# A planner that counts a longer landing time for the loads and stores of weights that are made early

## The chip, the core and the metric

The kernel runs on one core of a Trainium2 chip. The metric is the device time of one execution in microseconds; less is better. In the profile PE is TensorE (matmul), DVE is VectorE, ACT is ScalarE, POOL is GpSimd and SP is SyncE, whose queue issues every DMA of this kernel.

## What is computed

A banded attention with block summaries, a gated feed-forward network and a second network with a tanh residual, one after the other, in fp32 (cut to what matters):

```python
# attention: batch 2, 8 heads, 768 positions, head size 64; blocks of 32, window 16
k_sum = k.reshape(B, H, nb, block, D).max(axis=3)
v_sum = v.reshape(B, H, nb, block, D).mean(axis=3)
scores_l = np.where(abs(i - j) < window, scale * q @ k.T, -1e9)
scores_s = scale * q @ k_sum.T + log(block)
attn = softmax(concat(scores_l, scores_s)) @ concat(v, v_sum)
# feed-forward 1: 1536 tokens, 512 -> 1536 -> 512
xn = x / rms(x) * rms_g
x = (silu(xn @ w_gate) * (xn @ w_val)) @ w_out
# feed-forward 2: 512 -> 2048 -> 512
h = x @ w_in
out = (h - tanh(h)) @ w_out2
```

The weights of both networks come as 8-byte floats and are turned to fp32 on the chip.

## The kernel before

**Work.** The 1536 tokens are twelve tiles of 128, in three groups of four. Attention is done in 24 units (a tile and half of the heads). The first network (kind "a") goes over the three groups, each with twelve steps, one for each 128 columns of the hidden layer; a step is 4 + 4 first products (gate and value, into the PSUM tiles `mid`) and 4 second products (into the accumulators `bank`). Every fp32 product is three matmuls (L778 to L780) of rounded parts, high and low: `ih`, `il` for gate and value weights, `oh`, `ol` for the out weights, `hh`, `hl` for the hidden values. The units of the next group run between the steps of the one before. The second network (kind "b") takes the hidden columns in eight pairs for each group: seven products with added and subtracted blocks in place of eight, then the second products.

**Weights.** `widen` (L720) loads 8-byte weights into one of two `raw` buffers (L734) and turns them into fp32 with ACT (L736) and DVE (L737, L738). `split` makes the rounded parts, high by ACT (L753) and low by DVE or POOL (L755). For the second network's out weights `make_out` (L994) does both early, during the first network's second group: load into `raw` (L1002), ACT L1004, DVE L1005 and L1006, then the high part by ACT (L1007) and the low part by DVE or POOL (L1011) into the one buffer `op` (printed as `hi`), and two stores of 256 KB to device memory (L1015, tensors `ko`). There are sixteen such weights, so 16 loads and 32 stores; the next L1007 can't write `op` before both stores have landed. The second network later fetches the parts again (`fetch_outs`, L1020) into `oh` and `ol`, of which there are three each, shared with the first network's splits. `make` does the like for the second network's first weights (tensors `ki`, L1060 to L1082).

**What sets the order.** Nothing is written in the order in which it runs. Every instruction is an `Op` with an engine, an estimated time, the operations that it comes after, the buffers (`Slot`) that it takes, and a due time. `Plan.order` runs a clock over them: on each engine the ready operation with the smallest latest start is taken next, if its buffers are free. The order that comes out is written into the engines' instruction streams, and each engine then works strictly in that order on the chip, waiting by semaphores. A wrong estimate therefore breaks nothing, but lets an engine stand before an instruction whose input is not there while later ones could run. A DMA of `mb` MB is estimated at `mb * 2.78` us (L371); `lag` (L98) adds 1.0 us until its reader may start, and 1.3 us between an engine's end and a DMA. A buffer counts as free for an engine 0.2 us (`LAT`) after its last user's end, for a DMA 1.3 us after.

Of the kernel before, what the change touches and what calls it, by code (L numbers as in the profile page):

```python
# [16 lines left out]
NT, DM = B * S, H * D  # L17
# [3 lines left out]
P = 128  # L21
# [29 lines left out]

OPS = 7
AHEAD = 20.0
GROWS = (slice(32, 64), slice(64, GROW + 2 * NB))


def r32(ap):
    return ap.bitcast(F32)
# [11 lines left out]
class Op:  # L70
    def __init__(self, eng, us, fn, after, slots, due, rank, port):
# [5 lines left out]
        self.after = [o for o in after if o is not None]  # L77
        self.start = self.late = None


class Plan:

# [14 lines left out]

    def lag(self, a, b):  # L98
        if a.eng == "dma":
            return 0.0 if b.eng == "dma" else 1.0  # L100
        if b.eng == "dma":
            return 1.3
        if a.eng == b.eng:
            return {"pe": 0.0, "dve": 0.13}.get(a.eng, 0.05)
        return self.LAT

    def order(self, filler=None, gap=0.0):
# [58 lines left out]
        while events:  # L166
# [3 lines left out]
            for eng, queue in list(ready.items()):  # L170
# [28 lines left out]
                for s in o.slots:  # L199
                    if s.pool and s.index is None:  # L200
                        t, s.index = s.pool.idle.pop(0)
                        if s.most:
                            s.pool.held += 1
                    s.left -= 1
                    if s.pool and not s.left:
                        insort(s.pool.idle, (end, s.index))
                        insort(events, end + self.LAT)
                        insort(events, end + 1.3)
                        if s.most:
                            s.pool.held -= 1  # L210
                for q in o.then:
# [45 lines left out]
def kernel(  # L257
# [109 lines left out]
        o.alts = dict(rest)  # L367
        return o

    def dma(mb, fn, *after, **kw):  # L370
        return plan.op("dma", mb * 2.78, fn, after, **kw)  # L371

    def cols(tl, t):
        for i, (t0, n) in enumerate(GROUPS):
# [42 lines left out]
    def summary(b, hb, *after):  # L417
# [3 lines left out]
        def load(dst, src, rank):  # L421
            parts = 2 if b else 1
            n = NP * S // parts
            return [
                dma(
                    n * P * 4e-6,
                    lambda c=slice(j * S + i * n, j * S + i * n + n): nc.sync.dma_start(dst[:, c], src[:, c]),
                    *after,
                    rank=None if b else rank + 3 * hb,
                )  # L430
                for i in range(parts)
            ]
# [62 lines left out]
    def one_unit(t, hb, due, tag="att"):  # L495
# [7 lines left out]


        def load_part(c, rank=None):
            return dma((c.stop - c.start) * P * 4e-6, lambda: nc.sync.dma_start(u[:, c], units[i, :, c]), slots=[u], rank=rank)

        if i < 2:
            load = load_part(slice(0, VO), (-99, -96.65)[i])
# [467 lines left out]
    def dma_both(n, pick, slots, kept, *after):  # L977

        ops = []
        for s, k in zip(slots, kept):  # L980
            def go(s=s, k=k):
                here, there = r32(s[:, :n]), r32(k)
                nc.sync.dma_start(*((here, there) if pick else (there, here)))

            o = dma(n * P * 4e-6, go, *after, chain.get(("ld", n == DM)) if pick else None, slots=[s])
            if pick:
                chain["ld", n == DM] = o
            ops.append(o)
        return ops
# [4 lines left out]
    def make_out(f, due):  # L994
# [4 lines left out]
        du = lambda: d[:].bitcast(U32)  # L999
        src = w2[f].bitcast(U32)  # L1000
        gate = first_ops["a", 0]
        ld = dma(0.524, lambda: nc.sync.dma_start(raw[:], src[:, 1024:2048]), chain.get("raw"), slots=[raw])  # L1002
        chain["raw"] = ld
        a = act(0.58, lambda: nc.scalar.activation(d[:], w(1).bitcast(F32), AF.Prelu, scale=2.0 ** -112, alpha=-(2.0 ** 32)), ld, *gate, slots=[raw, d])  # L1004
        a = dve(0.34, lambda: nc.vector.tensor_scalar(du(), du(), 3, None, ALU.logical_shift_left), a, slots=[d], port=True)  # L1005
# [4 lines left out]
        def rest(on):  # L1010
# [1 line left out]

        z = flex({"pool": (1.32, lambda: rest(nc.gpsimd), True), "dve": (0.61, lambda: rest(nc.vector), True)}, a, slots=[d, o])
        stored_o[f] = [
            dma(DM * P * 4e-6, lambda i=i: nc.sync.dma_start(r32(keep_o[n][j][i]), o[:, i * 512:(i + 1) * 512]), x, slots=[o], due=due)  # L1015
            for i, x in enumerate((a, z))
        ]
        made_o.extend(stored_o[f])
# [1 line left out]
    def fetch_outs(n):  # L1020
        outs = []
        for j in (1, 0):
            w = [slot("oh"), slot("ol")]
            o = dma_both(DM, True, w, keep_o[n][j], *stored_o[2 * n + j])
            outs.insert(0, (*w, [o]))
        return outs

# [328 lines left out]
```

## Time and profile before

| | |
|---|---|
| median of 3 runs | 673.54 us (670.91, 673.54, 906.21) |
| the profiled execution | 674.08 us, its span 672.4 us |
| PE busy | 656.7 us (98%), 3714 matmuls |
| DVE busy | 451.4 us (67%) |
| ACT busy | 333.1 us (50%) |
| POOL busy | 48.9 us (7%) |
| DMA | 136.51 MB, mean 203 GB/s |

The span is the time from the first to the last instruction of the profiled execution. Busy time is the union of an engine's instructions; the ends of matmuls are modelled, so what a matmul costs is better read from the distance of starts. A wait is an engine's idle time together with the instruction, or the DMA, that ended it.

### The profile page before, as it was taken

Reading aid. Unit: us, or ns where it says so; the run is one execution under the profiler, and the core shown is the slowest. Engines: PE = TensorE matmul, PEld = TensorE weight load, DVE = VectorE, ACT = ScalarE, POOL = GpSimd, SP = SyncE. Lnnn points to the kernel's source line nnn. Section 1 sums busy time; section 2 is a strip of 40 time slices with the busy share of each in tenths; the row PEclk is TensorE's granted clock in tenths of the full one; section 3 lists DMA queues with packets and bytes.
Section 4 is the critical chain, followed back from the end, with each engine's and each line's share of the span. In section 5 each row is a group of like instructions: output and inputs, shape, how many; then the busy total and the mean of one; then the engine's idle time right before and its main releaser. Section 6 shows DMA issues by size and latency. Waiting matters only on the chain.

```text
span 672.4 us, 10478 instructions
## 1 busy us (share of the span) xinstructions
PE 656.7 (98%) x3714; PEld 552.6 (82%) x3714; DVE 451.4 (67%) x1011; ACT 333.1 (50%) x688; POOL 48.9 (7%) x114
## 2 busy tenths in 40 slices
PE   8999999999999999999999999999999999999996
PEld 7997777888876778888878888888888888888885
DVE  5798987885876875549978547987583444445343
ACT  3995566774764755447645436444362222323222
POOL 2221222110112120000000000000000000000000
PEclk9999999999999999999999999999999999999999
DMA  9886564662477665000645017687768787888842
GB/s 342 325 298 238 177 203 145 194 197 84 129 236 245 204 200 202 0 1 1 234 157 157 0 68 294 235 304 272 253 230 288 267 282 267 282 305 276 268 167 94
DMA packets 52251, 136.51 MB, mean 203 GB/s; under 512 B 6200, under 2 KB 8680, under 8 KB 52200
## 3 DMA queue, kind: packets, MB, share of 16 engines
q1 hardware_dynamic: 52200, 135.86, 60.2%
q8 instruction: 29, 0.48, 0.3%
q14 instruction: 22, 0.18, 0.1%
HBM read 109.62 MB, written 26.21 MB: 202 GB/s over the span
## 4 chain that ended last, share of the span: by engine, by line
PE 58%; DMA 4%; DVE 4%; ACT 2%; issue 1%; SPq 0%; DVEq 0%; ACTq 0%
PE bank L778 12%; PE bank L780 12%; PE bank L779 12%; PE mid L778 7%; PE mid L779 6%; PE mid L780 6%; DMA raw<-in_w_dram 3%; DMA out_dram<-th 1%; PE bank L641 1%; DMA ko<-hi 1%; PE bank L547 1%; PE bank L598 1%; DVE wd L738 1%; PE bank L652 0%; ACT wd L736 0%
## 5 line engine op out<-in xcount | busy, mean ns | idle before, releaser
L778 PE MATMUL mid<-hi,ih 128*128 128x512 f32 (+1 forms) x304 | 121.7, 400 | 0.1
L779 PE MATMUL mid<-lo,ih 128*128 128x512 f32 (+1 forms) x304 | 116.7, 384 | 0.0
L780 PE MATMUL mid<-hi,il 128*128 128x512 f32 (+1 forms) x304 | 116.5, 383 | 0.0
L780 PE MATMUL bank<-oh,hl 128*128 128x512 f32 x192 | 75.7, 394 | 0.5 <-DVE hl L1164 0.5
L778 PE MATMUL bank<-oh,hh 128*128 128x512 f32 x192 | 75.9, 395 | 0.1
L779 PE MATMUL bank<-ol,hh 128*128 128x512 f32 x192 | 75.4, 392 | 0.0
L778 PEld LDWEIGHTS mid<-hi,ih 128*128 128x128 f32 x304 | 57.4, 189 | 12.8 <-issue 2.4
L780 PEld LDWEIGHTS mid<-hi,il 128*128 128x128 f32 x304 | 57.2, 188 | 12.1
L779 PEld LDWEIGHTS mid<-lo,ih 128*128 128x128 f32 x304 | 57.4, 189 | 9.8
L778 PE MATMUL bank<-hh,oh 128*128 128x512 f32 (+1 forms) x152 | 60.3, 397 | 0.0
L779 PE MATMUL bank<-hl,oh 128*128 128x512 f32 (+1 forms) x152 | 58.2, 383 | 0.9 <-DVE hl L839 0.9
L780 PE MATMUL bank<-hh,ol 128*128 128x512 f32 (+1 forms) x152 | 58.1, 382 | 0.0
L753 ACT CAST ih<-wd 128x512 fp32r<-128x512 f32 x76 | 46.3, 618 | 23.3 <-PE mid L779 15.2
L755 DVE TENSOR_TENSOR il<-wd,ih 128x512 fp32r<-128x512 f32 x71 | 49.1, 700 | 3.8 <-ACT ih L753 3.4
L832 DVE TENSOR_TENSOR th<-th,mid 128x512 f32<-128x512 f32 (+1 forms) x38 | 25.0, 657 | 35.2 <-PE mid L780 35.0
L736 ACT ACTIVATE wd<-raw 128x512 f32<-128x512 f32 x46 | 30.9, 674 | 32.3 <-DMA raw<-in_w_dram 32.0
L1147 ACT ACTIVATE lo<-lo 128x512 f32<-128x512 f32 (+1 forms) x48 | 25.0, 523 | 39.8 <-DVE lo L1126 39.8
L780 PEld LDWEIGHTS bank<-oh,hl 128*128 128x128 f32 x192 | 36.1, 188 | 9.9 <-DVE hl L1164 1.5
L1147 ACT ACTIVATE lo<-mid 128x256 f32<-128x256 f32 x24 | 9.2, 383 | 67.6 <-PE mid L780 67.6
L778 PEld LDWEIGHTS bank<-oh,hh 128*128 128x128 f32 x192 | 36.2, 188 | 3.6 <-ACT hh L1163 0.3
L779 PEld LDWEIGHTS bank<-ol,hh 128*128 128x128 f32 x192 | 36.0, 188 | 3.6
L1151 DVE TENSOR_TENSOR lo<-lo 128x512 f32<-128x512 f32 (+1 forms) x48 | 26.6, 556 | 15.4 <-ACT lo L1147 15.4
(172 smaller groups left out, 1470.8 us busy)
## 6 DMA issues: line engine op xcount, KB each, us to landing
raw<-in_w_dram SPq DMA_DIRECT2D x62, 512.0 KB, 4.2
wd<-ki SPq DMA_DIRECT2D x32, 512.0 KB, 6.0
oh<-ko SPq DMA_DIRECT2D x48, 256.0 KB, 2.9
ol<-ko SPq DMA_DIRECT2D x48, 256.0 KB, 3.3
wd<-ki SPq DMA_DIRECT2D x32, 384.0 KB, 4.8
pad<-in_units_dram SPq DMA_DIRECT2D x19, 442.0 KB, 5.2
ko<-hi SPq DMA_DIRECT2D x32, 256.0 KB, 3.9
ki<-ih SPq DMA_DIRECT2D x7, 512.0 KB, 3.9
```

The costliest lines, as they stand in the source:

```text
L547: nc.tensor.matmul(ps[e][:, j * SC:(j + 1) * SC], q[r, j], k[r, j], start=(j == 0), stop=(j == NP - 1), skip_group_check=True,)
L598: nc.tensor.transpose(pt[:, h * P:(h + 1) * P], sc[:, m0:m0 + P], ident)
L641: nc.tensor.matmul(av[:, h * (D + 1):(h + 1) * (D + 1)], ph[:, h * P:(h + 1) * P], v[:, h], start=(h == 0), stop=False, skip_group_check=True,
L736: a = act(0.58, lambda d=d, w=w: nc.scalar.activation(d, w(k=1).bitcast(F32), AF.Prelu, scale=2.0 ** -112, alpha=-(2.0 ** 32)), ld, *after ...
L753: a = act(0.52, lambda c=c: nc.scalar.copy(wh[:, c], d[:, c]), dep, chain.get(tag), slots=[wh])
L755: on.tensor_tensor(wl[:, c], d[:, c], r32(wh[:, c]), ALU.subtract)
L778: nc.tensor.matmul(o, ah, bh, start=first, stop=False, skip_group_check=True)
L779: nc.tensor.matmul(o, ah, bl, start=False, stop=False, skip_group_check=True)
L780: nc.tensor.matmul(o, al, bh, start=False, stop=last, skip_group_check=True)
L832: a = dve(0.07 + 0.535 * v, lambda: nc.vector.tensor_tensor(th[:, :n], th[:, :n], m1[:, :n], ALU.mult), a, m1.done, slots=[m1, th])
L1147: o = act(us, lambda: nc.scalar.activation(out(), x(), AF.Tanh), *after, slots=slots)
L1151: return dve(us, lambda: nc.vector.tensor_tensor(out(), x(), z(), ALU.subtract), *after, slots=slots)
```

## The change

Each DMA operation gets a landing time of its own, `land`, in place of the fixed 1.0 us in `lag`. It is 1.0 (`LAND`) for all but the load and the two stores of `make_out`, which get 4.0 (`FAR`). A buffer whose last user is a DMA is given back `land - LAT` later than the DMA's estimated end; that holds for the stores of the output tiles (`th`) as well, with 1.0. And `fetch_outs` now also comes after `split_op["a", NF1 - 1]`, the splits of the first network's last weights in all three groups.

```diff
+LAND = 1.0
+FAR = 4.0
@@ class Plan, lag
         if a.eng == "dma":
-            return 0.0 if b.eng == "dma" else 1.0
+            return 0.0 if b.eng == "dma" else a.land
@@ Plan.order
                     if s.pool and not s.left:
-                        insort(s.pool.idle, (end, s.index))
-                        insort(events, end + self.LAT)
-                        insort(events, end + 1.3)
+                        seen = end + (o.land - self.LAT if o.eng == "dma" else 0.0)
+                        insort(s.pool.idle, (seen, s.index))
+                        insort(events, seen + self.LAT)
+                        insort(events, seen + 1.3)
@@
-    def dma(mb, fn, *after, **kw):
-        return plan.op("dma", mb * 2.78, fn, after, **kw)
+    def dma(mb, fn, *after, land=LAND, **kw):
+        o = plan.op("dma", mb * 2.78, fn, after, **kw)
+        o.land = land
+        return o
@@ make_out
-        ld = dma(0.524, lambda: nc.sync.dma_start(raw[:], src[:, 1024:2048]), chain.get("raw"), slots=[raw])
+        ld = dma(0.524, lambda: nc.sync.dma_start(raw[:], src[:, 1024:2048]), chain.get("raw"), slots=[raw], land=FAR)
...
-            dma(DM * P * 4e-6, lambda i=i: nc.sync.dma_start(r32(keep_o[n][j][i]), o[:, i * 512:(i + 1) * 512]), x, slots=[o], due=due)
+            dma(DM * P * 4e-6, lambda i=i: nc.sync.dma_start(r32(keep_o[n][j][i]), o[:, i * 512:(i + 1) * 512]), x, slots=[o], due=due, land=FAR)
@@ fetch_outs
-            o = dma_both(DM, True, w, keep_o[n][j], *stored_o[2 * n + j])
+            o = dma_both(DM, True, w, keep_o[n][j], *stored_o[2 * n + j], *split_op["a", NF1 - 1])
```

The line numbers of the changed kernel are 8 higher in the functions named here (L1004 is L1012, L1007 is L1015, L753 is L761, and so on). The order is the same on every engine up to the first made out weights, at the end of the first group.

ACT, in the second group's first half, around one attention unit (exponentials L575, copies L608 and L609 of its transposed scores). Before:

```order
L575 ACTIVATE pad_70<-pad_70,st_83 128x184 x4
L828 ACTIVATE th_101<-mid_81 128x512
L1004 ACTIVATE hi_1_1707<-raw_89 128x512
L608 COPY pad_70<-bank_78 128x512
L1007 CAST hi_1_1707<-hi_1_1707 128x512
L1004 ACTIVATE hi_1_1707<-raw_90 128x512
L609 COPY pad_70<-bank_78 112x256
L753 CAST ih_91<-wd_0_67 128x512 x2
```

And with the change, at the same unit:

```order
L1012 ACTIVATE hi_1_1707<-raw_89 128x512
L761 CAST ih_92<-wd_0_67 128x512
L583 ACTIVATE pad_70<-pad_70,st_83 128x184 x4
L836 ACTIVATE th_101<-mid_81 128x512
L616 COPY pad_70<-bank_78 128x512
L1015 CAST hi_1_1707<-hi_1_1707 128x512
L1012 ACTIVATE hi_1_1707<-raw_90 128x512
L617 COPY pad_70<-bank_78 112x256
L761 CAST ih_91<-wd_0_67 128x512 x2
```

Between the exponentials and the copy of the transposed scores one reader of a `raw` load has moved ahead of them.

DVE, in the third group, one step's hidden values (L832, then the low part `hl`, L839) beside the widening of the second network's weights (L737, L738). Before:

```order
L832 TENSOR_TENSOR th_101<-th_101,mid_82 128x512
L755 TENSOR_TENSOR il_93<-wd_0_68,ih_91 128x512
L737 TENSOR_SCALAR wd_0_67<-wd_0_67 128x512
L738 SCALAR_TENSOR_TENSOR wd_0_67<-raw_89,wd_0_67 128x512
L755 TENSOR_TENSOR ol_100<-wd_0_67,oh_97 128x512
L839 TENSOR_TENSOR hl_105<-th_101,hh_103 128x512
```

And with the change:

```order
L840 TENSOR_TENSOR th_101<-th_101,mid_82 128x512
L763 TENSOR_TENSOR il_93<-wd_0_68,ih_91 128x512
L745 TENSOR_SCALAR wd_0_67<-wd_0_67 128x512
L746 SCALAR_TENSOR_TENSOR wd_0_67<-raw_90,wd_0_67 128x512
L847 TENSOR_TENSOR hl_105<-th_101,hh_103 128x512
L763 TENSOR_TENSOR il_93<-wd_0_68,ih_91 128x512
L763 TENSOR_TENSOR ol_100<-wd_0_68,oh_97 128x512
```

The low part of the out weights, `ol`, has moved behind the low part of the hidden values; on ACT their high parts (L753, L837) have changed places in the same way.

SP, at the end of the train of made out weights. Before, two fetches (L983 of `ko`) stand there, and two more in the middle of the train:

```order
L1015 DMA ko_1_0_154<-hi_1_1707 128x512
L1015 DMA ko_1_1_155<-hi_1_1707 128x512
L983 DMA oh_96<-ko_0_0_124 128x512
L983 DMA ol_99<-ko_0_1_125 128x512
L734 DMA raw_90<-in_w_dram 128x1024
```

And with the change, the first fetches, after the last widening load of the second network:

```order
L742 DMA raw_90<-in_w_dram 128x1024
L991 DMA wd_1_3302<-ki_0_108 128x1024
L991 DMA wd_1_3302<-ki_1_109 128x1024
L991 DMA wd_1_3302<-ki_0_108 128x768
L991 DMA wd_1_3302<-ki_1_109 128x768
L991 DMA oh_97<-ko_1_0_126 128x512
L991 DMA ol_100<-ko_1_1_127 128x512
```

The four fetches have moved behind all of the first network's splits and behind four loads of kept `ki` weights. The first widening load of the second network now stands before the stores of the last three made weights (before, of the last two), so the train's end overlaps more of the widening.

## Rows read from the trace of the kernel before

**Rows 1.** Windows: stretch, sum, busy us (instructions) of PE, PEld, DVE, ACT, POOL, clock, DMA.

```profile
60.00:176.00 116.00, 114.93 (x630) 93.25 (x629) 93.36 (x215) 73.84 (x150) 20.43 (x44) 1.00 0.49 152
176.00:262.00 86.00, 83.05 (x422) 64.59 (x421) 63.59 (x144) 52.19 (x109) 14.57 (x21) 1.00 0.71 230
262.00:300.00 38.00, 38.00 (x202) 30.98 (x201) 19.36 (x48) 17.88 (x38) 1.48 (x4) 1.00 0.05 14
...
336.00:360.00 24.00, 23.13 (x99) 18.32 (x98) 18.37 (x33) 11.69 (x21) 0.00 (x0) 1.00 0.49 154
...
580.00:600.00 20.00, 19.47 (x121) 16.74 (x120) 10.62 (x24) 7.02 (x16) 0.00 (x0) 1.00 0.92 314
...
665.00:672.40 7.40, 1.51 (x7) 0.93 (x5) 1.28 (x3) 1.45 (x4) 0.00 (x0) 0.79 0.40 142
```

**Rows 2.** Waits of PE, whole span: us in total, times, longest.

```profile
PE bank L598 <- DVE st L561: 2.0, 2, 1.4
...
PE bank L652 <- ACT pad L609: 1.4, 1, 1.4
...
PE bank L779 <- DVE hl L839: 0.9, 1, 0.9
...
PE bank L780 <- DVE hl L1164: 0.5, 1, 0.5
```

**Rows 3.** Waits of all engines from 176 to 262 us.

```profile
ACT hi L1004 <- DMA raw<-in_w_dram: 11.9, 5, 4.2
...
ACT hi L1007 <- DMA ko<-hi: 7.4, 4, 2.7
```

**Rows 4.** Issue to landing, source views of L1002, L1015 and L734, in turn.

```profile
DMA to landing us min/median/max: 3.9/4.9/6.9
...
DMA to landing us min/median/max: 2.0/3.9/6.0
...
DMA to landing us min/median/max: 3.4/4.0/7.9
```

**Rows 5.** Timeline of ACT at 204 us: start, us, instruction [idle before].

```profile
203.94 0.66 ACT L1004 ACTIVATE hi<-raw 128x512 f32<-128x512 f32 x1 [3.31 <-DMA raw<-in_w_dram]
204.50 0.36 ACT L609 COPY pad<-bank 112x256 f32<-112x256 f32 x1
```

**Rows 6.** Timelines of DVE and, last row, POOL from 216 us.

```profile
216.59 1.70 DVE L1011 TENSOR_TENSOR hi<-hi 128x512 fp32r<-128x512 f32 x1 [2.01 <-DMA ko<-hi]
...
221.44 0.68 DVE L1011 TENSOR_TENSOR hi<-hi 128x512 fp32r<-128x512 f32 x1
...
216.46 1.29 POOL L755 TENSOR_TENSOR il<-wd,ih 128x512 fp32r<-128x512 f32 x1
```

**Rows 7.** The chain that ended last, pieces in order of time: start, us, what.

```profile
211.47 5.03 DMA ko<-hi
...
220.04 0.33 PE bank L598
...
249.98 0.44 PE bank L598 x4
```

**Rows 8.** Timelines of ACT and DVE from 348 us.

```profile
347.91 0.67 ACT L736 ACTIVATE wd<-raw 128x512 f32<-128x512 f32 x1 [4.16 <-DMA raw<-in_w_dram]
...
349.69 0.68 DVE L755 TENSOR_TENSOR ol<-wd,oh 128x512 fp32r<-128x512 f32 x1
```

**Rows 9.** Timeline of ACT at 586 us.

```profile
586.35 0.37 ACT L1189 COPY th<-bank 128x256 f32<-128x256 f32 x1 [2.27 <-DMA out_dram<-th]
```

**Rows 10.** The page's DMA issues: transfer, count, KB each, median us to landing.

```profile
oh<-ko SPq DMA_DIRECT2D x48, 256.0 KB, 2.9
...
wd<-ki SPq DMA_DIRECT2D x32, 512.0 KB, 6.0
```

**Rows 11.** Timelines of SP and PE at the start of the second network.

```profile
407.64 1.27 SPq L983 DMA_DIRECT2D wd<-ki  x3
...
417.75 0.40 PE L778 MATMUL bank<-oh,hh 128*128 128x512 f32 x1
```

More of the change, by code (lines that the diff above doesn't have):

```diff
@@ L78, in __init__ @@
         self.start = self.late = None
+        self.land = 1.0
 class Plan:
@@ L429, in load @@
                     rank=None if b else rank + 3 * hb,
+                    land=LAND if b else 1.0,
                 )
@@ L505, in load_part @@
         def load_part(c, rank=None):
-            return dma((c.stop - c.start) * P * 4e-6, lambda: nc.sync.dma_start(u[:, c], units[i, :, c]), slots=[u], rank=rank)
+            return dma((c.stop - c.start) * P * 4e-6, lambda: nc.sync.dma_start(u[:, c], units[i, :, c]), slots=[u], rank=rank, land=LAND if i >= 8 else 1.0)
         if i < 2:
```

## The prediction

> **What bounds the kernel now.** Read first the windows by stage [rows 1]: the columns that matter are PE's busy time against the length of the window. From 60 us on PE is busy 114.93 of 116.00, 83.05 of 86.00, 38.00 of 38.00, 23.13 of 24.00 and 19.47 of 20.00 us; the stretches left out there are full but for 0.4 us in all. So TensorE's own stream sets the time, at the full granted clock (1.00 in every one of these windows), and all that another order can win before the last output tiles is 1.07 + 2.95 + 0.87 + 0.53 + 0.4 = 5.8 us of visible idle time. The last window (1.51 of 7.40 us) is the copying out and storing of the last tiles, whose order the change leaves as it is, and the first 60 us are planned alike too: the first difference on any engine stands in the train of the early made out weights.
>
> Second, who ended PE's waits [rows 2]. Four rows matter: PE L652 waited once, 1.4 us, for ACT L609; PE L598 waited twice, 2.0 us, of which one wait is 1.4; PE L779 once, 0.9, for DVE L839; PE L780 once, 0.5, for DVE L1164. None of these names a DMA. Third, therefore, what the engines named had waited for. In the stretch from 176 to 262 us, where the weights are made, ACT stood 11.9 us before L1004 for the raw load and 7.4 us before L1007 for the store of the weights made before [rows 3].
>
> Fourth, each stall from near by. At 200 us [rows 5]: ACT waits 3.31 us for the raw load, runs L1004 at 203.94 and only then L609, 0.36 us of work, for which PE had stood 1.40 us. L609 had nothing to wait for itself; it stood behind L1004 on an engine that works in order. At 216 us [rows 6] it is DVE: L1011 waited 2.01 us for the store's landing, then took 1.70 us, and the score maxima L561 that PE's transposes L598 need stood behind it. At 348 us [rows 8] ACT waits 4.16 us before L736, a load for the widening of the second weights, and L837, L839 and PE's second products come after it. At 586 us [rows 9] ACT waits 2.27 us before L1189 for a store of an output tile, with L1163 behind it.
>
> Why the engines come to a transfer that is not there: the planner counts a load of 0.524 MB as 0.524 x 2.78 = 1.46 us plus 1.0, so the order expects it 2.46 us after its start. In the trace the sixteen raw loads take 3.9 to 6.9 us from issue to landing, median 4.9 [rows 4]. For a store it counts 0.73 us and gives the buffer back 0.2 later; in the trace the 32 stores take 2.0 to 6.0, median 3.9 [rows 4].
>
> **The change part by part.** No instruction, byte or tile is added or removed; what changes is the order, so the sum has only waits in it, and it is made against the profiled execution's own 674.1 us (its span 672.4 and 1.7 around it), which lies 0.5 above the median of the runs, 673.5.
>
> Load and store of the made out weights with FAR = 4: the plan now puts L1004 5.46 us after its load's start instead of 2.46, and L1007 and L1011 4.73 us after a store's start instead of 0.93. Both allowances lie above the medians of 4.9 and 3.9 [rows 4] and below the maxima. At the first stall the change's ACT order still has an L1004 directly before L609, but the L1004 that stood before L608 is gone: the train is one load behind, and the raw load comes earlier relative to its reader. I take the wait of 1.4 away in full; bounds 0 (the load takes 6.9 again, 1.4 more than allowed) and -1.4. **Term 1: -1.4.** At the second stall L1011 now expects its store 4.73 us after the start; the store of that place took 5.03 [rows 7], so by the same time it would be late by 0.3 instead of 2. **Term 2: -1.4**, bounds 0 and -1.4.
>
> There is a rule that speaks against term 2. The L1011 in question took 1.70 us where the next one took 0.68, and POOL's L755 ran from 216.46 for 1.29 us beside it [rows 6]; about 1.0 us of the stall is this stretching. The Trainium skill (page "SBUF — State Buffer", section "SBUF: two separate sides") says that VectorE and GpSimd share one pair of ports as a lock that one holds for a whole instruction while the other stands still. By that rule a longer latency in the plan would return 0.4 and not 1.4, and the sum below would be 671.1 instead of 670.1; the row agrees that the operation was stretched. I keep 1.4 because the changed order has five such POOL operations in this train instead of seven.
>
> Transposes at ACT's pace: four transposes L598 that follow the four exponentials L575 one by one take 0.33 us each; where ACT is ahead, four take 0.44 in all [rows 7]. Three such groups stand between 197 and 233 us, 3 x 3 x 0.22 = 2.0 us, which the windows count as busy. ACT is late there because of its waits, and half of it should go. **Term 3: -1.0**, bounds 0 and -2.0.
>
> The first outs' fetch moved behind the last split of the gate and value weights (L1024 gets split_op["a", NF1 - 1]): before, two pairs of the three oh and ol buffers were filled in the middle of the first part and sat there, so from then on one pair served all splits of the out weights. Now three serve, the ol split is no longer pressing, and the planner puts hl (L839) before ol (L755) on DVE and hh (L837) before oh (L753) on ACT at 348 us. Each of these steps is 0.6 us [rows 8], and the 0.9 stall shrinks by the DVE one; the 4.16 wait for the load stays, as widening loads keep 1.0. **Term 4: -0.6**, bounds 0 and -0.9. On SP the fetch now stands behind four loads of the first kept pair; they land in 6.0 us and the fetch in 2.9 [rows 10]. Before, the loads of that kind issued at 407.64 [rows 11], since the last split hung on the single buffer; with three buffers the split and with it these loads come up to a step earlier (twelve products of 0.69 us, about 8 us), and the first reader is PE at 417.75 [rows 11]. 6.0 + 2.9 from 400 or even from 408 is before 417.75: cost 0; were the cover gone, 1 to 3 us.
>
> Buffers freed by a DMA are given back 0.8 us later (output tiles th are the ones that matter): at 586 us L1163 now stands before the third L1189 on ACT, and so no longer behind its 2.27 us wait. **Term 5: -0.5**, bounds 0 and -0.5 [rows 2, 9].
>
> What is late next: the train is longer. Three widening loads of the second weights now have their reader L736 among the last attention units and the first steps of the third group, still planned at 2.46 us, where 4.0 is the median [rows 4]. That stretch had no idle PE time [rows 1] and no such reader. Each can cost from 0 to 0.9, the price of the same wait at 348 us; I let one of three hit. **Term 6: +0.9**, bounds 0 and +2.7.
>
> Sum: 674.1 - 1.4 - 1.4 - 1.0 - 0.6 - 0.5 + 0.9 = **670.1 us**.
>
> **The rivals.** *The wait moves.* Landing times scatter from 3.9 to 6.9 [rows 4], so a fixed 5.46 is missed by the slow ones; terms 1 and 2 come back by half at other places (1.4), term 3 does not come (1.0), all three widening readers hit (+1.8): 670.1 + 4.2 = 674.3 at the bad end, about 673 in the middle. For it: the structure L1004 before L609 is still there, and an L1011 that a POOL operation stretches by 1.0, as in [rows 6], would be one form of it. Against: medians are inside both allowances.
>
> *Nothing happens.* The stalls belong to the order of ACT and DVE around them and not to the allowance: 674.
>
> *Slower than before.* The last six of the sixteen weights now are made after the place where the old train ended, beside the attention units of the third group and its steps, in a stretch where PE had no gap [rows 1]. If every late load there stops PE like the one of term 1, that is 6 x 1.4 = 8.4: 674.1 + 8.4 = 682.5, or 679.7 with terms 1 and 2 gained, so about 680. It decides from the third stall on (3 x 1.4 against the 4.0 won). For it: ACT and DVE work in order there too. Against: in that stretch DVE is busy 19.36 and ACT 17.88 of 38.00 us [rows 1], so they are behind PE nowhere.
>
> **How the numbers follow.** Forecast 0.52, the wait moves 0.25, nothing 0.10, slower 0.13. The likeliest case has its own range: all gains in full and no term 6 give 674.1 - 1.4 - 1.4 - 2.0 - 0.9 - 0.5 = 667.9; term 6 at 2.7 and half of term 3 gone give 672.4. Median runs lie 0.5 below the profiled one and the lowest of before 3.2 below, so the range goes down to 665.5; upward it takes in the two cases without gain and a third of the slower one, to 677.5. A measurement of this kernel can tell about 2%, 13.5 us. Faster by that would need 660, more than all idle time of PE that the rows show: 0.02. Slower by that, 687, would need nine stalls of 1.4: a quarter of the slower case, 0.03. Within: 0.95.
>
> **What would show it.** Right: in 176 to 262 us PE's idle time falls from 2.95 to under 1; ACT's waits before L1004 (11.9) and L1007 (7.4) in the train fall to a few us; PE L652 and L598 no longer among PE's waits; at the place of 348 us a wait of about 0.3; none at 586. Wrong: PE waits for ACT or DVE between the old end of the train, 262 us, and 300; the raw loads' landing median above 5.5; a wait of PE at the first second product of the last part; or gaps gone and the span the same, which would mean that these gaps were cushions and PE pays at a later wait.

## The result and the profile after

| | before | after |
|---|---|---|
| median of the runs, us | 673.83 | 664.68 (664.26 to 666.70) |
| the profiled execution, us | 674.08 | 664.52 |
| its span, us | 672.4 | 662.4 |
| ratio after / before | | 0.9873, interval 0.9843 to 0.9902 |

The change saves 1.3%, some 8.5 us by the ratio. The median of before still counts one slow run of 906.21 us, which the ratio leaves out; without it that median is 673.54. The saving is within the 2%, as forecast; but the forecast was 670.1, and the measured time lies 0.8 us under the low end of its range. The direction and the place were right; the gain is about twice as large as the 4.0 us of the sum.

The windows of the changed kernel, columns as in [rows 1]; PE's busy time is to be held against the length of the stretch:

```profile
60.00:176.00 116.00, 115.85 (x637) 94.55 (x636) 94.95 (x218) 73.54 (x149) 19.22 (x44) 1.00 0.50 155
176.00:262.00 86.00, 86.00 (x460) 70.08 (x459) 60.41 (x143) 53.80 (x111) 10.53 (x20) 1.00 0.54 171
262.00:300.00 38.00, 38.00 (x195) 30.73 (x195) 28.11 (x63) 25.11 (x51) 2.11 (x3) 1.00 0.43 137
...
336.00:360.00 24.00, 24.00 (x105) 19.27 (x104) 18.99 (x34) 12.82 (x22) 0.00 (x0) 1.00 0.46 139
...
400.00:408.00 8.00, 7.75 (x64) 7.36 (x62) 4.38 (x11) 4.24 (x9) 0.00 (x0) 1.00 0.89 329
...
570.00:590.00 20.00, 20.00 (x128) 17.77 (x127) 10.72 (x24) 7.02 (x16) 0.00 (x0) 1.00 0.91 312
```

In 176 to 262 us the idle time of PE has gone from 2.95 us to nothing, and the stretch now holds 460 matmuls where it held 422: a first hint, though work has moved by some us too, that more than 2.95 us of idle time was won. The gaps at 348 and 586 us are gone too, and a small new one (0.25) stands at 403. Waits of PE over the whole span, changed kernel, first rows (us in total, times, longest):

```profile
PE bank L555 <- POOL wd L527: 1.6, 2, 1.3
PE mid L1262 <- DVE idle L1257: 1.0, 1, 1.0
PE bank L786 <- DVE lo L1134: 0.6, 3, 0.3
PE bank L700 <- DVE pad L707: 0.6, 1, 0.6
```

None of the four rows of [rows 2] is left. ACT's waits for raw loads and for stores of made weights [rows 3], 11.9 and 7.4 us, have no row any more between 170 and 300 us. The train's transfers also land earlier than in [rows 4]; the widening loads, whose allowance is unchanged, do not. Issue to landing in the changed kernel, of the raw loads (L1010), the stores (L1023) and the widening loads (L742), in turn:

```profile
DMA to landing us min/median/max: 3.6/4.1/5.8
...
DMA to landing us min/median/max: 2.0/2.7/5.0
...
DMA to landing us min/median/max: 3.4/4.1/7.9
```

**Where the 10.0 us between the two profiled spans went** is told by the start of the k-th of the 3714 matmuls, and not by idle time, since idle time misses matmuls that PE runs at another engine's pace. The third column is a second execution of the unchanged kernel (the first experiment below):

| start of matmul, us | before | before again | after |
|---|---|---|---|
| 1000, ahead of the train | 169.13 | 167.28 | 167.41 |
| 1400, behind it | 249.93 | 247.60 | 241.60 |
| 1800, ahead of the place of 348 us | 330.87 | 328.54 | 322.60 |
| 1900 | 355.34 | 352.95 | 345.96 |
| 2100, ahead of the second network's last part | 402.04 | 399.45 | 392.67 |
| 2200 | 417.51 | 414.89 | 408.56 |
| 3200, ahead of the place of 586 us | 580.37 | 577.76 | 571.43 |
| 3300 | 597.36 | 595.73 | 587.34 |

Distances between two marks, before less after: 6.6 us over the train (80.80 less 74.19), 1.1 at 348 us, -0.4 at the second network's last part, 1.1 at 586. The remaining 1.7 lies ahead of matmul 1000, where both orders are the same, and the second execution of before gains it as well (1.85): it is scatter of the start and no part of the change. Without it 8.3 us are left, close to the 8.5 of the ratio.

### The profile page after: what moved, and what is told of

It is laid out like the page before. It is cut to its first block, busy times and chain, and to the rows that moved or that the text cites. A ratio compares the mean times of both kernels' runs of the same rounds, so it can differ in the third digit from the quotient of the medians.

```text
span 662.4 us, 10467 instructions
## 1 busy us (share of the span) xinstructions
PE 651.8 (98%) x3714; PEld 552.5 (83%) x3714; DVE 449.3 (68%) x1013; ACT 334.2 (50%) x688; POOL 44.8 (7%) x112
## 4 chain that ended last, share of the span: by engine, by line
PE 88%; DMA 5%; DVE 3%; ACT 2%; SPq 0%; issue 0%; POOL 0%; ACTq 0%; DVEq 0%
PE bank L786 15%; PE bank L788 14%; PE bank L787 14%; PE mid L786 12%; PE mid L787 12%; PE mid L788 12%; PE bank L649 2%; PE bank L555 2%; PE bank L660 1%; DMA pad<-in_units_dram 1%; DMA raw<-in_w_dram 1%; PE bank L606 1%; DMA wd<-in_units_dram 1%; DMA wd<-in_ksum_dram 1%; DMA wd<-in_vsum_dram 1%; PE bank L700 1%
## 5 line engine op out<-in xcount | busy, mean ns | idle before, releaser
L761 ACT CAST ih<-wd 128x512 fp32r<-128x512 f32 x76 | 46.9, 619 | 24.0 <-PE mid L787 16.2
L583 ACT ACTIVATE pad<-pad,st 128x184 f32<-128x184 f32 x88 | 32.7, 442 | 9.9 <-DVE st L569 9.9
```

The lines of the kernel that those rows point to most:

```text
L583: nc.scalar.activation(s, s, AF.Exp, bias=st[:, 0, h:h + 1], scale=-1.0)
L761: a = act(0.52, lambda c=c: nc.scalar.copy(wh[:, c], d[:, c]), dep, chain.get(tag), slots=[wh])
```

## The experiments

All times are set against the kernel before, run beside it. "Train's waits" are the waits of ACT and DVE for raw loads and stores of made weights between 170 and 300 us; "PE idle" is that of 176 to 262 us; "train gain" is how much shorter than in the first profile of before the distance from matmul 1000 to 1400 is. The second execution of before shows what scatter that column has: 0.5. In the two orders due 4 us earlier the stretch holds other matmuls than in the rest, some 0.6 us more work (an estimate from the median distance of starts of each form), so their gain is rather 5.5 and 6.3.

| kernel | train's waits, us | PE idle, us | train gain, us | median, us | ratio, interval |
|---|---|---|---|---|---|
| before | 22.4 | 2.95 | 0 | 673.83 | |
| before again | 19.2 | 3.05 | 0.5 | 672.45 (one) | |
| fetch moved alone | 22.0 | 2.65 | 2.25 | 671.65 | 0.9975, 0.9961 to 0.9990 |
| latency and give-back | 0 | 0 | 6.6 | 666.57 | 0.9898, 0.9872 to 0.9923 |
| late give-back alone | 11.9 | 1.50 | 5.2 | 667.07 | 0.9908, 0.9883 to 0.9934 |
| short loads | 5.6 | 0.03 | 5.8 | 667.15 | 0.9925, 0.9898 to 0.9952 |
| no POOL in the train | 18.6 | 2.56 | 2.2 | 670.99 | 0.9977, 0.9954 to 1.0000 |
| before, due 4 us earlier | 10.7 | 0.44 | 4.95 | 669.60 | 0.9951, 0.9930 to 0.9972 |
| before, due 4 us later | 16.8 | 0.82 | 4.6 | 670.85 | 0.9977, 0.9957 to 0.9997 |
| after | 0 | 0 | 6.6 | 664.68 | 0.9873, 0.9843 to 0.9902 |
| after, due 4 us earlier | 0 | 0.00 | 5.8 | 664.60 | 0.9869, 0.9836 to 0.9903 |
| after, due 4 us later | 0 | 0.09 | 6.3 | 665.06 | 0.9876, 0.9843 to 0.9909 |
| latency for stores only | 2.6 | 0.02 | 5.7 | 666.66 | 0.9907, 0.9875 to 0.9939 |
| latency for loads only | 5.6 | 0.00 | 6.55 | 664.45 | 0.9864, 0.9829 to 0.9898 |
| FAR = 1.5 | 3.3 | 0.25 | 5.8 | 666.17 | 0.9896, 0.9855 to 0.9937 |
| FAR = 8 | 0 | 0.01 | 6.3 | 663.81 | 0.9864, 0.9828 to 0.9899 |
| after, with another buffer at the end | 0 | 0 | | 663.33 | 0.9853, 0.9817 to 0.9888 |

**Before again.** The unchanged kernel in a second profile, to see what one profile's numbers are worth.

> The kernel before once more, for a second profile. Theory 'landing' (the stalls come from loads and stores that land later than the plan counts): the same stalls at the same instructions, since the order is the same, but of other lengths, as landing times scatter; PE again idle for 2 to 4 us between 176 and 262 us and 0.5 to 1.2 us at 348 us. Rival 'chance' (the profiled execution of before was unlucky): these stalls are mostly gone and the span is near 667. Either way this shows whether the 1.7 to 2.1 us that the changed kernel was ahead at 75 us, before any difference in order, is scatter: then this profile's PE stands somewhere between the two there.

PE's waits, then the window of the train and DVE from 213 us:

```profile
PE bank L692 <- DVE pad L699: 1.7, 2, 1.2
...
PE bank L652 <- ACT pad L609: 1.4, 1, 1.4
PE bank L780 <- DVE hl L1164: 1.1, 1, 1.1
...
PE bank L779 <- DVE hl L839: 0.9, 1, 0.9
PE bank L598 <- DVE st L561: 0.4, 1, 0.4
```

```profile
176.00:262.00 86.00, 82.95 (x427) 64.88 (x426) 64.03 (x144) 53.93 (x112) 14.65 (x21) 1.00 0.69 227
```

```profile
213.01 1.71 DVE L1011 TENSOR_TENSOR hi<-hi 128x512 fp32r<-128x512 f32 x1 [1.00 <-DMA ko<-hi]
```

The stalls for ACT L609 and for L839 come again to the tenth. The one at L598 is 0.4 instead of 1.4: its store was late by 1.00 instead of 2.01 [rows 6], and PE paid exactly that much less. The one at 586 us is 1.1 instead of 0.5. And one place is new: at 238 us PE stands 1.2 us for DVE L699, which comes behind L1005 on DVE, which waits for ACT L1004, which waits for a raw load:

```profile
236.53 0.66 ACT L1004 ACTIVATE hi<-raw 128x512 f32<-128x512 f32 x1 [1.92 <-DMA raw<-in_w_dram]
```

```profile
237.22 0.43 DVE L1005 TENSOR_SCALAR hi<-hi 128x512 uint32<-128x512 uint32 x1 [3.43 <-ACT hi L1004]
237.56 0.75 DVE L699 SCALAR_TENSOR_TENSOR pad<-pad,st 128x512 f32<-128x512 f32 x1
```

So two stalls, place and size, come with the order in both executions. The other two differ in size, and a late load can stop PE at a place that another execution of the same order does not show.

**The parts alone.** The change has three parts: the latency of the train's transfers, the 0.8 us later give-back of buffers that a DMA frees, and the fetch moved behind the last split. Into the kernel before, the moved fetch alone:

```diff
-            o = dma_both(DM, True, w, keep_o[n][j], *stored_o[2 * n + j])
+            o = dma_both(DM, True, w, keep_o[n][j], *stored_o[2 * n + j], *split_op["a", NF1 - 1])
```

> Of the change only the moved fetch: fetch_outs also waits for the last split; landing times are counted as before. Theory 'landing': the stalls in the train of made weights stay (PE idle 2 to 4 us between 176 and 262 us, ACT before L1004 some 10 us); only the stall at 348 us shrinks: ratio 0.998 (0.995 to 1.000). Rival 'buffers' (the gain comes from three free oh and ol buffers instead of one): most of the gain, ratio 0.990.

And the changed kernel without it (the same line the other way round):

> Of the change only the landing times (4.0 for the load and stores of the made weights, and buffers given back later); the fetch stays early. Theory 'landing': PE's idle time between 176 and 262 us goes to near 0 and that at 586 us too, the stall at 348 us stays: -6.6 - 1.1 us, ratio 0.989 (0.985 to 0.993). Rival 'buffers': ratio 0.997.

The moved fetch takes away the stall of 348 us, puts a small wait at 408, leaves the stall at 586 (0.47) and leaves the train's waits as they were (22.0): 0.25%. Of its 2.25 us of train gain 0.8 lie ahead of matmul 1185, up to which PE's order is that of before, and are scatter; the rest lies between there and matmul 1250, where the stall at 216 us stood: it has a shorter one (0.8) at 229 us instead. The second kernel has the latency together with the late give-back. It has no wait for the train's transfers, no idle time and the whole 6.6 us, keeps the stall of 348 (0.85), and has none at 586. So the train belongs to these two parts and 348 us to the fetch, as the prediction divided them.

**The late give-back alone.** The changed kernel with FAR = 1.0 and without the moved fetch; what is left is the later give-back.

> Of the change only that a buffer whose last user is a DMA is given back 0.8 us later in the plan, with 1.0 us of landing for all and the fetch early as before. Theory 'landing': it reorders the copies of the output tiles, so the stall at 586 us goes (1.1 us by the starts of matmuls), and it gives the made weights' stores 0.8 us more, which is too little beside 3.9: ratio 0.997 (0.994 to 1.001). Rival 'any reordering does it' (the train's stalls go with any other order of the same work): 0.990.

This was a miss: 0.9908, where little was expected. The stall at 586 us is gone, which the moved fetch alone had left standing, so that one is the give-back's. But 5.2 us of the train are won as well, though the plan gives its loads no more time and its stores only 0.8 us before their buffer is free, and the waits are still there:

```profile
ACT hi L1015 <- DMA ko<-hi: 7.1, 5, 3.3
...
ACT hi L1012 <- DMA raw<-in_w_dram: 2.5, 1, 2.5
...
DVE hi L1019 <- DMA ko<-hi: 2.3, 3, 1.2
```

PE still idles there (1.50 us), at other places than before: 0.9 at 181 us and 0.6 at 257. With 11.9 us of waits left, the gain looks like that of another order, in which less of what PE needs next stands behind a late transfer; this run does not separate the order from the 0.8 us. Nor do the intervals tell 0.9908 from the 0.9898 with the latency. That raised the question of how much of the gain any other order would bring.

**Is it late transfers at all?** Before's order, word for word, with the raw loads a quarter as large, so that they land sooner (the weights made from them are not the reference's):

```diff
-        ld = dma(0.524, lambda: nc.sync.dma_start(raw[:], src[:, 1024:2048]), chain.get("raw"), slots=[raw])
+        ld = dma(0.524, lambda: nc.sync.dma_start(raw[:, 0:256], src[:, 1024:1280]), chain.get("raw"), slots=[raw])
```

> The order of the kernel before, instruction for instruction; only the sixteen raw loads of the early made out weights bring a quarter of their bytes (128 KB instead of 512), so the made out weights are wrong. Theory 'landing': the loads land after about 2.5 us, what the plan counts; ACT's wait before L1004 (11.6 us in the train) falls under 3, PE's stall at L652 (1.4 us) goes, and the stores' stalls may shrink with the emptier queue: PE idle between 176 and 262 us under 1.5 us, ratio 0.994 (0.991 to 0.997). Rival 'order' (the instruction order itself is bad there, whatever lands when): stalls as before, ratio 1.00.

Landings of its raw loads, then of its stores; its waits of 170 to 300 us that name these transfers; its window:

```profile
DMA to landing us min/median/max: 2.3/2.5/3.5
...
DMA to landing us min/median/max: 2.0/2.6/4.1
```

```profile
ACT hi L1004 <- DMA raw<-in_w_dram: 2.2, 2, 1.9
...
ACT hi L1007 <- DMA ko<-hi: 2.0, 2, 1.4
...
DVE hi L1011 <- DMA ko<-hi: 1.4, 1, 1.4
```

```profile
176.00:262.00 86.00, 85.97 (x455) 69.33 (x455) 66.28 (x148) 55.92 (x115) 16.42 (x23) 1.00 0.51 166
```

With the order untouched and the loads landing at 2.5 us, about the 2.46 that the plan counts, both stalls of the train are gone, and 5.8 of the 6.6 us that the change won there are back; the stalls at 348 and 586 us stay (0.87 and 1.10). The stores became faster too, 3.9 to 2.6, without a byte less, so this run doesn't separate loads from stores. What it shows is the cause: in before's order, late transfers are what the train loses its time to.

**The shared port.** Before's order with the train's seven POOL operations run by DVE in the same places.

```diff
+                if o.eng == "pool" and "dve" in o.alts and 165.0 < o.start < 260.0:
+                    o.alts["dve"][1]()
+                    continue
```

> The order of the kernel before, but the seven POOL operations of the train (six low parts L755 and one L1011) run on DVE at the same place of the order. Theory 'landing': the stretched L1011 and L1006 (1.7 us for 0.7) are normal again, but DVE has 7 x 0.69 us more; PE's stalls stay between 2 and 4 us, ratio 1.000 (0.997 to 1.004). Rival 'ports' (the stall before L598 comes from POOL holding DVE up): the waits for DVE L561 go, ratio 0.997.

ACT and DVE still wait 18.6 us, the stall for ACT's copy stays (1.1), the one at L598 is 0.4 (now for ACT's exponentials), 0.9 us stand at the new place of before again, and the ratio is 0.9977, at the edge of no change. The 0.4 alone doesn't decide, since before again has it as well, with the stretching. The short loads decide it, since the stretched operation is still there, DVE first and then POOL:

```profile
210.13 1.71 DVE L1011 TENSOR_TENSOR hi<-hi 128x512 fp32r<-128x512 f32 x1
...
210.01 1.28 POOL L755 TENSOR_TENSOR il<-wd,ih 128x512 fp32r<-128x512 f32 x1
```

The same 1.7 us beside the same POOL operation, and PE doesn't wait at all. The three executions make a row: store late by 2.01, PE waits 1.4; late by 1.00, PE waits 0.4; not late, 0. The stretching is as it was in each; what PE pays follows the store, once 0.6 us of lateness have been used up.

**Luck of the order.** The making of the weights due 4 us earlier, and 4 us later, in the kernel before; this changes nothing but the order.

```diff
-                make_out(f, begin[1] + (begin[2] - begin[1]) * (f + 1) / NF2)
+                make_out(f, begin[1] - 4.0 + (begin[2] - begin[1]) * (f + 1) / NF2)
```

> The kernel before with the due times of the early made out weights' stores 4 us earlier, which gives another order of the same work with the same estimates of landing. Theory 'landing': the train still stops ACT and DVE at transfers that are not there (ACT before L1004 and L1007 over 10 us together), PE idle 2 to 5 us between 176 and 262 us, ratio 1.000 (0.996 to 1.005). Rival 'luck' (the order of before is an unlucky draw and nearly any other is better, as the run with the 0.8 us alone suggests): PE idle under 1.5 us, ratio 0.993.

> The same with due times 4 us later. Theory 'landing': as with the earlier due times, ratio 1.000 (0.996 to 1.005). Rival 'luck': 0.993.

Waits of the first:

```profile
ACT hi L1007 <- DMA ko<-hi: 7.6, 6, 3.0
...
ACT hi L1004 <- DMA raw<-in_w_dram: 3.1, 2, 1.9
```

ACT and DVE still wait 10.7 and 16.8 us in all, but PE idles only 0.44 and 0.82, where 2 to 5 had been expected: another miss, and the rival "luck" was nearer. The train is 4.95 and 4.6 us shorter in these two profiles, but the medians gain less (0.9951 and 0.9977): the profiled execution of the first was the fastest of its ten, 667.07 against a median of 669.60. The same two shifts with the change:

> The changed kernel with due times of the made weights' stores 4 us earlier: another order, same allowances. Theory 'landing and slack': with the allowance no engine waits for the train's transfers, so the order does not matter: no PE wait over 0.3 us between 176 and 262 us, ratio 0.987 (0.985 to 0.990). Rival 'luck' (the changed order is a good draw among orders): PE idle of 0.4 to 1.5 us there, ratio 0.989 to 0.992.

> The same with due times 4 us later. Theory 'landing and slack': as the changed kernel, 0.987 (0.985 to 0.990). Rival 'luck': 0.989 to 0.992.

Both as the change itself: no wait for the train's transfers, PE idle 0.00 and 0.09, ratios 0.9869 and 0.9876. So without the latency the train depends on which order the plan happens to fall into (PE idle 2.95, 2.65, 1.50, 0.82, 0.44 in five orders: before, the moved fetch, the late give-back, and the two shifts), and with it all three orders are good. The order of before was the worst of its five; with the shifted due times the kernel before would have been 0.2 to 0.5% faster, and by these ratios the change would have shown 0.8 to 1.0% instead of 1.3.

**Loads or stores.** The latency taken from the loads, then from the stores (`land=FAR` removed from one line each):

> The changed kernel with the longer landing for the made weights' stores alone; the load is counted with 1.0. Theory 'landing and slack': since the stores space the train out (one buffer, held until they land), raw loads are issued far ahead of their readers anyway, and ACT waits for loads little: 0 to 4 us; PE idle 0 to 0.7 us, ratio 0.988 (0.985 to 0.990). Rival 'the load is all': PE idle 1.5 us or more, ratio 0.991 or worse.

> The changed kernel with the longer landing for the made weights' load alone; their stores are counted with 1.0 again (but the buffer given back 0.8 later). Theory 'landing and slack' (a late transfer stops ACT or DVE, and PE pays only where what stands behind has no slack; the allowance ends the waits themselves): ACT waits before L1015 for stores for some 5 to 10 us, none before L1012 for loads; PE idle between 176 and 262 us 0.3 to 1.5 us; ratio 0.989 (0.986 to 0.992). Rival 'the load is all': as the changed kernel, 0.987, no waits for stores.

With the latency for stores only, one raw load is waited for (2.6 us); for loads only, stores are waited for three times (4.7 us on ACT). PE pays for neither (0.02 and 0.00; 0.3 to 1.5 had been expected of the second). Either one is enough to clear the train in these two orders. The first ratio, 0.9907, lies just outside what was expected of it. Between it and 0.9864 the intervals overlap, and the profile of the former has a stall of 0.7 at 72 us, ahead of any difference; nothing is read from that.

**How long.** FAR = 1.5, less than what the transfers take, and FAR = 8, more than any took:

> The changed kernel with 1.5 us instead of 4.0 for the made weights' load and stores. Theory 'landing and slack' (waits end only where the allowance is near the landing; below that PE pays by chance of what stands behind): ACT waits for raw loads and stores again, 5 to 15 us in the train, PE idle there 0.3 to 2 us, ratio 0.990 (0.987 to 0.994). Rival 'any value over the old one': as the changed kernel, no PE wait over 0.3 us in the train, 0.987.

> The changed kernel with 8.0 us. The train then takes about twice as long in the plan and runs into the third group and the widening of the second network's weights. Theory 'landing and slack': no wait for the train's transfers, and no cost while the train still ends before the second network needs it: ratio 0.987 (0.984 to 0.991). Rival 'too long costs': the widening loads start late and PE waits at the second network's start by 1 to 5 us, ratio 0.990 to 0.996.

FAR = 1.5 was expected to keep 5 to 15 us of waits and kept 3.3: a miss, as the stores land at 3.7 instead of 3.9 and the order is another. The range of one value says little here, for the same reason as above. FAR = 8 stretches the train to 351 us (last store; 293 in the changed kernel, 259 before) and costs nothing:

```profile
176.00:262.00 86.00, 85.99 (x456) 69.66 (x456) 55.23 (x133) 49.91 (x104) 11.00 (x20) 1.00 0.40 129
```

Its stores land at a median of 2.0 us. The slower rival, in which weights made late stop PE, would have grown with the length; even at twice the allowance there is nothing of it.

**What still waits.** At the end of the changed kernel DVE copies an output tile into a buffer that a store has to free first. With a free buffer of another pool for the last tiles:

```diff
-                ob = slot("th")
+                ob = slot("tb" if end and i > 1 else "th")
```

> The changed kernel, and the last two output tiles are copied into two buffers that the last pair has done with instead of into the two th buffers, whose stores have yet to land. In the changed kernel's last 7.4 us ACT and DVE wait about 2 us for these stores before the third tile's copies. The copies then follow PE's last products directly: 1.4 to 2.0 us less, ratio 0.985 (0.982 to 0.988) against the kernel before. Rival: the last stores land no earlier because four are in flight together, 0 to 0.5 us, 0.987.

DVE in the last window, changed kernel, and then this one:

```profile
657.55 0.42 DVE L1198 COPY th<-bank 128x256 f32<-128x256 f32 x1 [1.99 <-DMA out_dram<-th]
```

```profile
655.66 0.42 DVE L1198 COPY lo<-bank 128x256 f32<-128x256 f32 x1 [0.26 <-PE bank L788]
```

The wait of 1.99 is gone and the copy starts 1.9 us earlier; the span is 660.4 instead of 662.4. The median, 663.33, is the lowest of all kernels here, but its interval (0.9817 to 0.9888) overlaps with that of the change, so it is a likely gain of about 1 us and no proven one.

## Where the prediction was right, and where it failed

**The bound.** Right: PE's stream at the full granted clock sets the time, and what was won was time on PE. The step that failed is the one that sizes the gains and the low end of the range: "all that another order can win" is not the visible idle time of 5.8 us. After the scatter is taken off, 8.3 were won. Time in which PE ran at another engine's pace counts as busy and was won as well; only term 3 allowed for it, and for half.

**Terms 1 and 2** (1.4 each) held. Both waits are gone, and by the starts of the matmuls these places gave 1.56 and 1.61 (the second only 0.58 in before again). ACT at the first place, changed kernel:

```profile
197.80 0.67 ACT L1012 ACTIVATE hi<-raw 128x512 f32<-128x512 f32 x1 [0.76 <-DVE hi L1019]
...
199.09 0.38 ACT L617 COPY pad<-bank 112x256 f32<-112x256 f32 x1 [0.62 <-PE bank L611]
```

The making step still stands ahead of the copy, as the prediction saw, but it waits 0.76 for DVE and no longer 3.31 for the load, and the copy now waits for PE (0.62) instead of PE for it. On term 2 the Trainium skill (page "SBUF — State Buffer", section "SBUF: two separate sides") spoke for 0.4. The trace agrees with the page that the operation is stretched beside POOL's (1.71 against 0.68 in three executions), but the rows decided for 1.4: the stretch without the late store costs nothing (short loads). In the changed kernel no L1019 on DVE meets such a POOL operation; all fifteen take 680 to 694 ns.

**Term 3** (1.0) is the largest step that failed. The mechanism was right, the halving wasn't: with no wait of ACT for a raw load or a store of made weights left, none of the groups of transposes runs at ACT's pace. The one of [rows 7], 0.33 for one, is in the changed kernel's chain

```profile
212.17 0.44 PE bank L606 x4
```

and ten transposes at 0.23 less (0.34 from start to start in before, 0.11 here) give 2.3 us against the 1.0 of the term. In before again seven run so, with the moved fetch alone two. The group at 197 us shows how they hang on ACT's waits: in before, before again and the moved fetch ACT waits 2.31, 1.56 and 1.06 us for a store ahead of it, and three, one and none of its transposes are slow. Smaller pieces of the same kind, matmuls that the windows count as busy, bring about 1.1 more. So the train gave 6.6 instead of 3.8 (1.56 + 1.61 + 2.3 + 1.1).

**Term 4** (0.6) was 1.1. ACT and then DVE at the place of 348 us, changed kernel:

```profile
337.22 0.67 ACT L744 ACTIVATE wd<-raw 128x512 f32<-128x512 f32 x1 [2.83 <-DMA raw<-in_w_dram]
```

```profile
339.80 0.69 DVE L847 TENSOR_TENSOR hl<-th,hh 128x512 fp32r<-128x512 f32 x1
...
341.00 0.69 DVE L763 TENSOR_TENSOR ol<-wd,oh 128x512 fp32r<-128x512 f32 x1
```

The hidden values' low part now goes ahead of the weights' low part, as predicted, a step of 0.6. The shorter wait for the load (2.83 instead of 4.16) is not needed for the rest. With the moved fetch alone the stall is gone as well, and a wait of the same 4.16 a step later costs PE nothing:

```profile
352.35 0.66 ACT L736 ACTIVATE wd<-raw 128x512 f32<-128x512 f32 x1 [4.16 <-DMA raw<-in_w_dram]
```

```profile
355.19 0.40 PE L778 MATMUL bank<-hh,oh 128*128 128x512 f32 x1
```

PE's second products start 2.84 us after the reader there; in before it is 1.80 (349.71 against 347.91), in the changed kernel 4.31 (341.53 against 337.22). The term had held that distance constant; what moved the reader forward against PE was not isolated.

**Term 5** (0.5) was 1.1 by the starts of the matmuls; the visible wait was the smaller part, and in before again it was 1.1 by itself. Cause as stated: the run with the late give-back alone has no such stall, the moved fetch alone has.

**Term 6** (+0.9) was 0. The three readers that it names come among the last attention units and the first steps of the third group, and none waits for its load; the first of them starts at 288.28 us, then:

```profile
290.68 0.66 ACT L744 ACTIVATE wd<-raw 128x512 f32<-128x512 f32 x1
...
294.57 0.68 ACT L744 ACTIVATE wd<-raw 128x512 f32<-128x512 f32 x1
```

So no load was late for them, though the plan counts only 2.46 us. Later readers do wait, four of them up to 333 us, the longest 1.79, as readers of the kernel before do in its third group (0.51 to 2.19 ahead of the place of 348 us):

```profile
326.66 0.66 ACT L744 ACTIVATE wd<-raw 128x512 f32<-128x512 f32 x1 [1.79 <-DMA raw<-in_w_dram]
```

And PE waited nowhere from 250 to 335 us. The price of 0.9 was borrowed from the place of 348 us, where PE's next product stood behind the reader; here the late loads cost PE nothing.

**Not foreseen** (+0.4, where the text on term 4 had put the cost of the moved fetch at 0): the first splits for the second network's last part now stand ahead of its products. PE at 403 us, changed kernel:

```profile
403.58 0.39 PE L786 MATMUL bank<-pad,hi 128*128 128x256 f32 x1 [0.25 <-DVE lo L1134]
```

The moved fetch alone shows the same wait.

**The balance.** The forecast changed the time by 4.0 and the trace by 8.3: term 3 and its smaller pieces account for 2.4 of that 4.3, term 6 for 0.9, terms 4 and 5 for 1.1, terms 1 and 2 for 0.4, less the 0.4 not foreseen. The remaining 1.1 of the miss of 5.4 belongs to no term: the sum starts from an execution whose start was 1.7 us late, and the interval of the ratio alone is 6.6 to 10.6 us of gain. The range's low end, 665.5, allowed for all gains in full, but in full by the same idle times. It doesn't follow from its own parts either: 667.9 less the 3.2 by which the lowest run lay below the profiled one is 664.7.

**Rivals.** The wait didn't move: PE idle 0.00 in 176 to 262 and 262 to 300 us, and no PE wait names ACT in the train. "Nothing" falls with the short loads, which clear the train with the order unchanged. "Slower" falls with the third window: the last weights are made beside a full PE, DVE 28.11 and ACT 25.11 of 38.00 us busy, and PE has no gap; FAR = 8 shows the same for twice the length. What none of the rivals had was a case in which the gain is larger, because each was built on visible idle time.

**What stays open.** How the 8.5 us divide between the allowance and a luckier order has no single answer: by the two shifted orders of before, 1.6 to 3.3 us would have come from a shift alone, and the late give-back alone, with little more allowance, gave 6.2, the stall at 586 us included. Shorter stores with the order of before were not tried.

## What to carry to other kernels

Where a plan puts instructions in order on engines that work in order, count a transfer at no less than the median of its measured landing under the kernel's own load: allowances under it left the engines waiting (22.4 us in before, 3.3 at FAR = 1.5), with everything queued behind, while an allowance of twice the change's cost nothing here. Whether PE pays for such a wait is a matter of the order. Size a stall by the distance between the starts of the matmuls ahead of it and behind it, since matmuls that run at another engine's pace count as busy (3.4 of the 6.6 us). And before a gain is put down to a new planning rule, shift an unrelated due time with and without the rule: the spread of the unshifted side says how much was luck.

## What the runs showed of the hardware

Landing times fell where the same transfers were spread out, and this wasn't expected. With the same bytes in the same count, the raw loads went from a median of 4.9 us to 4.1 and the stores from 3.9 to 2.7, while the rate in 176 to 262 us fell from 230 to 171 GB/s and that in 262 to 300 rose from 14 to 137; at FAR = 8, with 129 GB/s in the first stretch, loads took 3.8 and stores 2.0. The page of the changed kernel has the medians of all such issues:

```profile
ko<-hi SPq DMA_DIRECT2D x32, 256.0 KB, 2.7
...
raw<-in_w_dram SPq DMA_DIRECT2D x62, 512.0 KB, 3.9
```

The allowance therefore helps twice: the reader comes later, and the transfer comes sooner. The short loads show it from the other side, where the stores land at 2.6 beside smaller loads. That the sharing of the DMA engines is the cause is argued from these rates, and no run isolates it.

Two executions of one order can also differ by 1.7 to 2 us by 75 us into the span (matmul 500 starts at 77.50 in the one and 75.48 in the other), where ACT waits 7.3 against 5.8 us for widening loads between 56 and 76 us.
